# One of four vector sums moved to an accumulating DMA inside SBUF, with the steps put in a new order

## The chip, the cores and the metric

The kernel runs on one core of a Trainium2 chip. The metric is the device time of one execution in microseconds (us); lower is better. Five engines work side by side, each through its own queue of instructions in order: PE (TensorE, matrix products), DVE (VectorE), ACT (ScalarE), POOL (GpSimd) and SP (SyncE). The last two are used here almost only to issue DMA transfers. An engine that has to wait for another holds up everything behind that wait in its own queue.

## The reference

Two parts follow each other: a channel attention over `q`, `k`, `v` (4 batches, 6080 tokens, 256 channels) and a feed-forward block of width 2048 on its result.

```python
qn = q / (np.linalg.norm(q, axis=1, keepdims=True) + 1e-06)
kn = k / (np.linalg.norm(k, axis=1, keepdims=True) + 1e-06)
s = kn.transpose(0, 2, 1) @ qn / tau          # 256 x 256 for each batch
a = softmax(s)
x = (v @ a).reshape(24320, 256)
h = x @ w_in                                  # 24320 x 2048
g = 0.5 * h * (1.0 + np.tanh(c * (h + 0.044715 * h * h * h)))
return g @ w_out                              # 24320 x 256
```

## The kernel before

**The two products.** The attention matrix is multiplied into `w_in` once for each batch (`aw`, 256 x 2048), so that `h = v @ aw` is one product for each block of 512 tokens. There are 12 blocks in a batch, the last of 448 tokens, and 48 in all; `n` is the block's number. The *first product* makes `h` and GELU makes `g` of it (bf16, in SBUF). The *second product* is `g @ w_out`, taken transposed, with `w_out` as the stationary operand.

**Both products use a form of Strassen and Winograd**: a 2 by 2 product of blocks with 7 products in place of 8, for sums that other engines make. In the first product this is done for one to three sets of four feature chunks for each block (the steps `w0...`, `w1...`, `w2...`, among them the matmuls `w0m1` to `w0m7`); the rest is done plainly (`g0`, `g3`, ..., four matmuls of 512 columns each, with GELU `G0`, `G3`, ...). In the second product it is done for all blocks. Write G(f,t) for the quarter of `g` with features half f and tokens half t, and W(h,f) for the quarter of `w_out` with output half h. The kernel before makes on DVE:

- T1 = G(0,1) - G(0,0) (`sums_1`, step `T1a`, one instruction of 2048 elements)
- T2 = G(1,1) - T1, T3 = G(1,1) - G(0,1), T4 = T2 - G(1,0) (`sums_2`, steps `T2a`, `T2b`, `T3a`, ..., two halves of 1024 elements each)

and seven products (`product`, steps `M1A`, `M1B` to `M7A`, `M7B`, four matmuls of 256 columns each): M1 to M3 read `g` itself, M5 reads T1, M6 reads T2, M7 reads T3 and M4 reads T4. The sums of `w_out` are made once at the start (`prep_wout`, steps `pF0`, `pS3`, ...).

**Buffers.** `g` has two buffers of `[128, 16, 512]`, T1, T2 and T3 one each, T4 two. The first GELU of block n+2 can write only when the last reader of block n's `g` is through.

**What sets the order.** Nothing reorders the steps: the list `ORDER` holds one string of steps for each window, a window being the time of one block, and `WINDOW` says which string a block uses (five of them serve twice). The program runs through these strings and hands each step to its engine's queue. A step such as `M7A-1` belongs to the block before. Besides the two products the windows hold the work for the next batch's attention matrix: loads of `q` and `k` (`lq`, `lk`, issued by POOL, with a cast from f32 to bf16), squares on ACT (`qsq`, `ksq`), sums of squares on DVE (`f1` to `f4`), rows of the 256 x 256 Gram matrix on PE (`row0`, ...). `v` is cast to bf16 by a DMA from DRAM to DRAM issued by POOL (`lv`) and then loaded transposed by a DMA issued by SP (`lt`); `vs` makes the sums of it on DVE. A load of `lq`, `lk` or `lv` is held back until the last matmul of a `g` or `w..m` step ahead of it in the list (`GATE`). SP also issues the stores of the output, four for each block.

A set of the first product is a chain across engines: after matmul `m6` DVE adds (`ap`, L618) before `m7` may write the same bank (L597), and ACT copies (`cq`, `y5`) come ahead of that.

**The tail.** After the last matmul of the last block (`M3B` in the last string) DVE still adds (`a12`, L742), transposes (`c12`, `c22`, L751), and four stores (`sA`, L804) go out.

Of the kernel before, what the change touches and what calls it, by code (L numbers as in the profile page):

```python
# [18 lines left out]
def kernel(  # L19
# [75 lines left out]
    def load_one(b, c, which, gate=None):  # L95
        r0, n = chunks_of(b)[c]
        t = qkp.tile([128, 8, 256], BF16, tag="qk"[which])
        src = (q, k)[which]
        after(nc.gpsimd.dma_start(
            out=t[:, 0:n, :],  # L100
            in_=src[b, 0 : R * 128, :].rearrange("(p r) c -> p r c", r=R)[:, r0 : r0 + n, :]), gate)
        if with_rest(b, c):
            after(nc.gpsimd.dma_start(out=t[:REM, n, :], in_=src[b, R * 128 : N, :]), gate)
        qk_tiles.setdefault((b, c), []).append(t)
# [13 lines left out]
    def cast_first(st):  # L118
        for which in range(2):
# [6 lines left out]
            qk_tiles.setdefault((0, 0), []).append(t)  # L126
# [366 lines left out]
    def gs(n):  # L493
        if n not in GS:
            GS[n] = gp.tile([128, FC, BLK], BF16, tag="g", name=f"g{n}")
        return GS[n]
# [32 lines left out]
    def gelu(n, p):  # L529
        cols = cols_of(n)  # L530
        nc.scalar.activation(gs(n)[:, 2 * p : 2 * p + 2, :cols], HP.pop((n, p))[:, :, :cols],  # L531
                             AF.Gelu_apprx_tanh)
# [74 lines left out]
    def set_step(n, i, what):  # L607
# [14 lines left out]
        if what == "Gq":  # L622
            nc.scalar.activation(  # L623
                gs(n)[:, 2 * pa : 2 * pa + 2, :c].rearrange("p u (t x) -> p t u x", t=2),
                QP.pop((n, i))[:, :, :c].rearrange("p t (u x) -> p t u x", u=2),
                AF.Gelu_apprx_tanh)
        if what == "Gr":
            nc.scalar.activation(gs(n)[:, 2 * pb : 2 * pb + 2, :hc], two(RB.pop((n, i))[:, :c]),  # L628
                                 AF.Gelu_apprx_tanh)
        if what == "Gx":  # L630
            nc.scalar.activation(gs(n)[:, 2 * pb : 2 * pb + 2, hc:c], two(XW.pop((n, i))[:, :c]),  # L631
# [24 lines left out]
    def prep_wout(what):  # L656
        if what == "pA11":
            nc.vector.tensor_copy(wc(A11), w_half(0, 0))
        if what == "pF0":
            WF.append(yout.tile([128, 32, 32], FP32, tag="ot", name="wf0"))  # L660
            nc.vector.tensor_add(WF[0], w_half(1, 0), w_half(1, 1))
        if what == "pS1":
            nc.vector.tensor_copy(wc(S1), WF[0])
        if what == "pF1":
            WF.append(yout.tile([128, 32, 32], FP32, tag="ot", name="wf1"))
            nc.vector.tensor_sub(WF[1], WF[0], w_half(0, 0))
# [8 lines left out]
        if what == "pS3":  # L675
            nc.vector.tensor_sub(wc(S3), w_half(0, 0), w_half(1, 0))
# [3 lines left out]
    def quarter(n, f, t, f0=0, f1=8):  # L680
        hc = cols_of(n) // 2
        return GS[n][:, f * 8 + f0 : f * 8 + f1, t * hc : t * hc + hc]
# [6 lines left out]

    def sums_2(n, i, half):  # L690
        hc = cols_of(n) // 2
        ts = TS.setdefault(n, {})
        if i not in ts:
            ts[i] = (t4p if i == 4 else tsp).tile([128, 8, BLK // 2], BF16, tag=f"t{i}",
                                                  name=f"t{i}_{n}")
        f0, f1 = half * 4, half * 4 + 4
        o = ts[i][:, f0:f1, :hc]
        if i == 2:
            nc.vector.tensor_sub(o, quarter(n, 1, 1, f0, f1), ts[1][:, f0:f1, :hc])  # L699
        if i == 3:  # L700
            nc.vector.tensor_sub(o, quarter(n, 1, 1, f0, f1), quarter(n, 0, 1, f0, f1))  # L701
# [6 lines left out]
    def product(n, i, halves=(0, 1), bank=None):  # L708
# [4 lines left out]
        for half in halves:  # L713
# [5 lines left out]
            for k in range(4):  # L719
                fc = half * 4 + k  # L720
                if i <= 3:
                    f, t = {1: (0, 0), 2: (1, 0), 3: (1, 1)}[i]
                    x = GS[n][:, f * 8 + fc, t * hc : t * hc + hc]
# [97 lines left out]
    with tc.manual_schedule():  # L821
# [93 lines left out]
        def step(what, n):  # L915
# [12 lines left out]
            elif what == "T1a":  # L928
                sums_1(n)
            elif what[0] == "T":  # L930
# [38 lines left out]
        for n in range(NN):  # L969
            for x in ORDER[WINDOW[n]].split():  # L970
# [4 lines left out]
WINDOW = [  # L975
    0, 1, 2, 3, 4, 5, 6, 7, 8, 9, 10, 11, 12, 13, 14, 15, 16, 17, 18, 19, 20, 21, 22, 23,
    24, 25, 26, 27, 28, 17, 18, 19, 20, 29, 30, 31, 32, 33, 34, 35, 36, 37, 38, 38, 39,
    40, 41, 42,
]
ORDER = [  # L980
    """g0 lv+3 aw3 G0 aw2 g1 ac2 ac3 aw4 G1 aw5 lq+1 ac4 g2 ac5 g3 G2 aw6 G3 g4 ac6 SW0 aw7 G4 g5
    lk+1 ac7 vtp G5 pA11 g6 vtc0 g7 vtc1 G6 T1a vtq G7""",
    """g0 vtr0-1 vtr1-1 lt+2 lv+3 g1 T2a-1 G0 T2b-1 M1B-1 G1 pF0-1 g2 g3 G2 pS1-1 w0m1+1 pF1-1
    lq+1 M1A-1 G3 g4 cq-1 pS2-1 pNA-1 g5 pS4-1 M6B-1 G5 M5A-1 pS3-1 M6A-1 G4 M5B-1 g7 vs+1
    y5-1 g6 ap-1 G7 T3a-1 lk+1 M3A-1 T3b-1 pA12-1 M7A-1 T4b-1 w0m5+1 M7B-1 w0cq+1 row0 ax-1
    row1 w0y5+1 M3B-1 T4a-1 G6 w0m6+1 M4B-1 c12-1 w0ap+1 M4A-1 qsq M2A-1 c21-1 M2B-1 row2
    c11a-1 M1B ksq T1a w0m2+1 w0m7+1 w0m3+1""",
    """g0 w0Gq T2a-1 lt+2 lv+3 row4-1 M5A-1 w0ax G0 M5B-1 T2b-1 M1A-1 f1-1 g4 cq-1 w0Gx T3a-1
    w0m4 G4 g3 lq+1 f2-1 vs+1 M6A-1 G3 g6 T4b-1 y5-1 M6B-1 c11-2 G6 g5 lt+3 lv+4 ap-1 T3b-1
    w0Gr M3A-1 G5 w0m5+1 T1a w0m1+1 row2 M7A-1 w0cq+1 lk+1 M3B-1 w0y5+1 M7B-1 c12-1 qsq w0m6+1  # L990
    c22-2 g7 w0ap+1 row5-1 T4a-1 row3-1 G7 w0m2+1 ax-1 w0m3+1 w0m7+1 f3-1 M2A-1 ksq M2B-1 T2a""",
    """g0 w0ax w0Gq row5-1 T2b-1 M4A-2 vs+1 M4B-2 G0 w0m4 g4 c21-2 w0Gr c11a-2 f1-1 g3 G4 SW1-3
    M1B-1 lq+1 G3 M5A-1 c22-2 M1A-1 f2-1 w0Gx w1m1 T3b-1 w1m5 M5B-1 w1cq T3a-1 g7 cq-1 T4a-1
    w1y5 lt+3 lv+4 row0-1 w1m6 y5-1 M6A-1 G7 w1ap M6B-1 row1-1 qsq ap-1 w1m2 w1m7 w1m3 w1ax
    row4-1 lk+1 M3A-1 T1a M7A-1 w1Gq w1m4 row3 M7B-1 w1Gr c11-2 M3B-1 f3-1 w1Gx row1 c12-1
    w0m1+1 w0m5+1 T4b-1 row2 w0cq+1 M2B-1 ax-1 M2A-1 w0y5+1 row3-1 ksq c11a-1 w0m6+1""",
    """g0 T3a-1 w0ap M4A-2 G0 M4B-2 T2b-1 M5B-1 T2a-1 w0m7 g3 c21-2 w0ax M1A-1 G3 f4-2 row0-1
    w0m4 M1B-1 c22-2 lq+1 w0Gr T3b-1 w0m3 w0m2 cq-1 w1m5 c11-2 M5A-1 w0Gq f1-1 M6B-1 w1m1 y5-1
    M6A-1 f2-1 w1cq g4 ap-1 lt+3 lv+4 w1y5 T4a-1 w1m6 G4 row4-1 w1ap M3A-1 M7A-1 vs+1 w0Gx
    M3B-1 ksq w1m7 f3-1 lk+1 w1m3 w1ax g7 T4b-1 M7B-1 G7 c12-1 w1m4 row1 ax-1 w1m2 f4-1 M2B-1  # L1000
    w1Gr w0m5+1 w1Gq T1a M2A-1 w0m1+1 M4A-1 w0cq+1 c11a-1 M4B-1 w0y5+1 T2a row5-1 w0m6+1 w1Gx
    M5A c21-1 w0ap+1""",
    """g0 qsq-1 T3a-1 M5B-1 T2b-1 w0m2 G0 M1A-1 f1-1 w0m7 M1B-1 y5-1 w0m3 w0ax cq-1 g3 w0Gq T4b-1
    M6A-1 lq+1 T3b-1 G3 w0m4 g4 vs+1 w0Gr M6B-1 G4 w1m5 ap-1 w1m1 row3-1 f2-1 lt+3 lv+4 row4-1
    w1cq M3A-1 M3B-1 w1y5 w1m6 w0Gx g7 w1ap ksq c12-1 lk+1 row2 w1m2 c22-2 w1m7 w1m3 w1ax
    M2A-1 G7 M7A-1 T4a-1 w1m4 row2-1 f3-1 row0-1 w1Gr M7B-1 T1a w1Gq row5-1 w0m1+1 w0m5+1
    M2B-1 ax-1 w0cq+1 c11-2""",
    """g0 w1Gx-1 T3a-1 w0y5 M4B-2 c11a-2 row0-1 T2b-1 G0 M4A-2 w0m6 c21-2 M5A-1 qsq-1 T2a-1 g3
    w0ap M1A-1 c22-2 M1B-1 f4-2 lq+1 w0m7 cq-1 M5B-1 w0ax G3 row3-1 M6B-1 T4b-1 M6A-1 y5-1
    c11-2 w0m2 w0Gx w0m4 T4a-1 row4-1 w0Gr row1-1 ap-1 w1m5 lt+3 lv+4 w0m3 T3b-1 w1y5 row5-1  # L1010
    w1m1 M3B-1 f1-1 w1cq M3A-1 w0Gq M7B-1 vs+1 w1m6 M7A-1 lk+1 w1ap g4 ksq ax-1 c12-1 w1m7
    w1m2 f2-1 M4B-1 w1ax G4 M4A-1 w1m3 c21-1 M2A-1 w1Gx f3-1 g7 w1Gq f4-1 w1m4 T1a M2B-1 G7""",
    """g0 w1Gr-1 T2a-1 M1A-1 G0 w0m5 c11a-2 w0m1 T4a-1 row3-1 M1B-1 w0cq T3b-1 M5B-1 w0y5 row5-1
    T2b-1 w0m6 cq-1 row0-1 qsq-1 g3 w0ap c11-2 lq+1 row2-1 T3a-1 w0m7 G3 M5A-1 c22-2 w0m2 w0ax
    w0m3 M6A-1 w0Gq T4b-1 M6B-1 w0m4 vs+1 w1m5 y5-1 row1-1 lt+3 lv+4 w0Gr g4 ap-1 w0Gx f1-1
    w1m1 G4 M7A-1 M3B-1 f2-1 M7B-1 w1cq lk+1 M3A-1 w1y5 w1m6 c12-1 qsq g7 w1ap M2B-1 ax-1 w1m7
    G7 c22-1 w1m3 w1m2 w1ax M4A-1 w1Gq T1a M4B-1 w1m4 w0m5+1 w1Gr M2A-1 c21-1 row2 w0y5+1
    c11a-1 row4-1 row4 T3a w0m1+1 M5B w0cq+1 f3-1 M1A T2a w1Gx M1B ksq f4-1 w0m6+1 row3 M5A
    w0ap+1""",
    """g0 c11-2 cq-1 T2b-1 y5-1 w0m7 G0 w0m2 w0ax w0m3 M6A-1 T3b-1 M6B-1 w0Gq g3 ap-1 f1-1 w0Gx  # L1020
    w0m4 G3 g4 vs+1 M7B-1 w0Gr T4a-1 M7A-1 G4 f2-1 w1m5 row1-1 ax-1 w1m1 M3B-1 T1a w1cq row5-1
    M3A-1 lt+3 lv+4 w1y5 w1m6 qsq g7 w1ap c22-1 M4A-1 c12-1 w1m7 ksq row5 w1ax w1m2 row0 row3
    T4b-1 M2A-1 w1m3 f3-1 G7 row2 w1m4 f4-1 M4B-1 M2B-1 w1Gr c21-1 w0m5+1 w1Gq c11a-1 row0-1
    M1B f1 row4 w0m1+1 row1 w0cq+1""",
    """lq+4 g0 f2-1 c11-2 w0y5 f3-1 M5B-1 T2a-1 G0 w0m6 M1A-1 w0ap M5A-1 gc T3a-1 g3 cq-1 w1Gx-1
    f4-1 w0m3 w0m2 T2b-1 w0m7 w0Gq ss w0ax M6B-1 T4a-1 y5-1 G3 M6A-1 sv w0m4 pow ap-1 g4 w0Gr
    T3b-1 w1m5 T4b-1 G4 M3B-1 lt+3 lv+4 w1m1 vs+1 M3A-1 w1cq M7A-1 kf w1y5 lk+4 w1m6 c12-1 g7
    w0Gx w1ap kr M7B-1 T1a G7 w1m7 w1m2 w1m3 krp w1ax w1Gq M2B-1 ax-1 w0m5+1 S0+1 M2A-1 w1Gx
    S1+1 w1m4 th0+1 M4A-1 c11a-1 w1Gr T3a M4B-1 th1+1 M5A c21-1 dn+1 w0m1+1 T2b""",
    """g0 w0cq rc0 w0y5 w0m6 M1B-1 G0 w0ap M5B-1 M1A-1 rc1 y5-1 w0m3 cq-1 w0m7 w0m2 T2a-1 g3 w0Gq  # L1030
    w0ax M6A-1 rc2 G3 lq+4 w0m4 M6B-1 T3b-1 g4 w0Gr ap-1 w0Gx w1m5 rc3 w1m1 lt+3 lv+4 M7B-1
    w1cq M3B-1 c22-2 w1y5 eT w1m6 M3A-1 G4 w1ap rsum+1 M7A-1 T4a-1 w1m7 g7 ax-1 rs+1 w1ax
    aw0+1 G7 c12-1 w1m2 w1m4 vs+1 w1m3 M4A-1 w1Gr ac0+1 M2B-1 w1Gq w0m1+1 T4b-1 w0m5+1 lk+4
    aw1+1 w0cq+1 c11-2""",
# [203 lines left out]
```

## Time and profile before

| | us |
|---|---|
| median of 3 timed runs (696.42 to 696.67) | 696.61 |
| the profiled execution, first to last instruction (its span) | 695.2 |
| median of the timed runs less the span: what lies around it | 1.4 |
| PE busy | 677.3 (97%) |
| DVE busy | 630.8 (91%) |
| ACT busy | 616.0 (89%) |
| POOL busy | 73.4 (11%) |
| DVE, the sums of T3 (L701), 96 instructions | 63.8 |
| mean granted TensorE clock | 0.998 |

The profiled execution has no other time of its own than its span; the 1.4 us between the span and the median is taken as what lies around it. The busy time of PE counts matmuls to their modelled ends, which overlap with the next, so 97% alone does not say that PE runs at its peak. For that one compares the starts of matmuls that follow each other. DMA transfers are shown at the instruction that issues them, with the time from issue to landing. Waits are put down to the engine, line or DMA that ended them.

### The profile page before, as it was taken

Reading aid. Unit: us, or ns where it says so; the run is one execution under the profiler, and the core shown is the slowest. Engines: PE = TensorE matmul, PEld = TensorE weight load, DVE = VectorE, ACT = ScalarE, POOL = GpSimd, SP = SyncE. Lnnn points to the kernel's source line nnn. Section 1 sums busy time; section 2 is a strip of 40 time slices with the busy share of each in tenths; the row PEclk is TensorE's granted clock in tenths of the full one; section 3 lists DMA queues with packets and bytes.
Section 4 is the critical chain, followed back from the end, with each engine's and each line's share of the span. In section 5 each row is a group of like instructions: output and inputs, shape, how many; then the busy total and the mean of one; then the engine's idle time right before and its main releaser. Section 6 shows DMA issues by size and latency. Waiting matters only on the chain.

```text
span 695.2 us, 14413 instructions
## 1 busy us (share of the span) xinstructions
PE 677.3 (97%) x5501; PEld 530.7 (76%) x5501; DVE 630.8 (91%) x1245; ACT 616.0 (89%) x894; POOL 73.4 (11%) x135
## 2 busy tenths in 40 slices
PE   3999999999999999999999999999999999999996
PEld 2857787777778777777777777777877888888785
DVE  3579998999998889999999889999999999999996
ACT  5389989999889999999988999999888999999993
POOL 4321101111001001101010100010000000000000
PEclk9999999999999999999999999999999999999999
DMA  9996888897478777747587777593563463453325
GB/s 240 207 269 98 160 141 126 114 150 109 65 144 126 130 120 105 122 80 121 91 138 121 119 120 126 97 141 53 83 99 69 77 103 61 81 103 59 54 39 89
DMA packets 161462, 79.07 MB, mean 114 GB/s; under 512 B 148448, under 2 KB 152160, under 8 KB 160672
## 3 DMA queue, kind: packets, MB, share of 16 engines
q0 software_dynamic: 14448, 39.72, 34.2%
q1 hardware_dynamic: 145696, 37.14, 31.8%
q10 hardware_dynamic: 1248, 1.28, 0.6%
q8 instruction: 43, 0.70, 0.4%
q14 instruction: 27, 0.22, 0.1%
HBM read 78.91 MB, written 36.57 MB: 166 GB/s over the span
## 4 chain that ended last, share of the span: by engine, by line
PE 95%; DMA 4%; DVE 0%; issue 0%; POOL 0%; ACT 0%; DVEq 0%; POOLq 0%
PE r L726 24%; PE h L521 22%; PE p L726 18%; PE rb L597 13%; PE qp L597 10%; PE G L248 5%; DMA t<-in_k_dram 2%; PE awp L461 2%; DMA t<-in_q_dram 1%; PE ss L282 0%; PE ss L275 0%; PE vt_ps L325 0%; PE rk L406 0%; PE warm L370 0%; DVE vT_pe L331 0%
## 5 line engine op out<-in xcount | busy, mean ns | idle before, releaser
L726 PEld LDWEIGHTS <-wcomb 128*128 128x128 bf16 x2688 | 261.9, 98 | 43.5 <-issue 0.2
L531 ACT ACTIVATE g<-h 128x1024 bf16<-128x1024 f32 (+1 forms) x178 | 179.9, 1014 | 16.4 <-PE h L521 13.9
L726 PE MATMUL r<-t,wcomb 128*128 128x256 bf16 (+1 forms) x1152 | 163.6, 272 | 0.1
L521 PE MATMUL h<-vT,aw 128*128 128x512 bf16 (+1 forms) x624 | 158.6, 377 | 0.0
L623 ACT ACTIVATE g<-qp 128x1024 bf16<-128x1024 f32 (+1 forms) x103 | 104.7, 1016 | 7.3 <-PE qp L597 5.8
L726 PE MATMUL p<-g,wcomb 128*128 128x256 bf16 (+1 forms) x760 | 108.0, 272 | 0.0
L521 PEld LDWEIGHTS <-aw 128*128 128x128 bf16 x712 | 69.2, 98 | 49.4 <-DVE aw L364 0.6
L597 PEld LDWEIGHTS <-sw 128*128 128x128 bf16 x824 | 80.2, 98 | 25.5 <-issue 1.3
L193 ACT ACTIVATE sq<-t 128x1536 bf16<-128x1536 bf16 (+4 forms) x59 | 79.2, 1359 | 6.2 <-DMA t<-in_q_dram 6.0
L618 DVE TENSOR_TENSOR qp<-rb,yw 128x512 f32<-128x512 f32 (+1 forms) x103 | 70.8, 688 | 12.3 <-PE rb L597 9.5
L597 PE MATMUL rb<-tv,sw 128*128 128x256 bf16 (+1 forms) x412 | 78.0, 271 | 0.2 <-DVE qp L618 0.2
L621 DVE TENSOR_TENSOR xw<-rb,yw 128x512 f32<-128x512 f32 (+1 forms) x103 | 69.5, 674 | 3.9 <-PE rb L597 2.4
L613 ACT ACTIVATE qp<-rb 128x512 f32<-128x512 f32 (+1 forms) x103 | 59.7, 580 | 11.9 <-PE rb L597 6.8
L597 PEld LDWEIGHTS <-aw 128*128 128x128 bf16 x618 | 60.3, 98 | 12.7 <-issue 0.7
L631 ACT ACTIVATE g<-xw 128x512 bf16<-128x512 f32 (+1 forms) x103 | 63.4, 626 | 1.3 <-DVE xw L621 1.2
L616 ACT ACTIVATE yw<-qp 128x512 f32<-128x512 f32 (+1 forms) x103 | 61.2, 594 | 3.7 <-PE qp L597 1.9
L699 DVE TENSOR_TENSOR t<-g,t 128x1024 bf16<-128x1024 bf16 (+1 forms) x96 | 63.4, 668 | 0.6
L701 DVE TENSOR_TENSOR t<-g 128x1024 bf16<-128x1024 bf16 (+1 forms) x96 | 63.8, 673 | 0.0
L703 DVE TENSOR_TENSOR t<-t,g 128x1024 bf16<-128x1024 bf16 (+1 forms) x96 | 63.6, 669 | 0.0
L628 ACT ACTIVATE g<-rb 128x512 bf16<-128x512 f32 (+1 forms) x103 | 61.2, 596 | 2.2 <-PE rb L597 1.7
L248 PE MATMUL G<-t 128*128 128x256 bf16 (+1 forms) x352 | 60.1, 279 | 0.1
L687 DVE TENSOR_TENSOR t<-g 128x2048 bf16<-128x2048 bf16 (+1 forms) x48 | 57.5, 1197 | 0.0
(137 smaller groups left out, 890.0 us busy)
## 6 DMA issues: line engine op xcount, KB each, us to landing
out_dram<-ot SPq DMA_DIRECT2D x174, 128.0 KB, 3.2
vb<-in_v_dram POOLq DMA_DIRECT2D x41, 256.0 KB, 4.2
t<-in_q_dram POOLq DMA_DIRECT2D x21, 384.0 KB, 4.9
t<-in_k_dram POOLq DMA_DIRECT2D x21, 384.0 KB, 5.8
wst<-in_moe_w_out_dram POOLq DMA_DIRECT2D x2, 1024.0 KB, 11.0
t<-in_q_dram POOLq DMA_DIRECT2D x3, 512.0 KB, 14.4
t<-in_k_dram POOLq DMA_DIRECT2D x3, 512.0 KB, 17.2
out_dram<-ot SPq DMA_DIRECT2D x12, 112.0 KB, 2.6
```

The source lines that it names most:

```text
L193: nc.scalar.activation(o, t[:np_, r, :], AF.Square)
L248: nc.tensor.matmul(G[b][:, jc, :], lhsT=qt[:np_, r, jc * 128 : jc * 128 + 128], rhs=kt[:np_, r, :], start=first and jc == 0, stop=jc == 1, ...
L521: mm = nc.tensor.matmul(hp[:, u, :cols], lhsT=AW[b][:, cc, fc * 128 : fc * 128 + 128], rhs=vt_tiles[n][:, cc, :cols], start=cc == 0, stop= ...
L531: nc.scalar.activation(gs(n)[:, 2 * p : 2 * p + 2, :cols], HP.pop((n, p))[:, :, :cols], AF.Gelu_apprx_tanh)
L597: GATE[0] = nc.tensor.matmul(acc[:, u * hc : u * hc + hc], lhsT=lhs[:, u * 128 : u * 128 + 128], rhs=rhs, start=m in (1, 5) and u == 0, st ...
L618: nc.vector.tensor_add(qp(n, i)[:, 1, :c], RB[n, i][:, :c], YW[n, i][:, :c])
L621: nc.vector.tensor_add(XW[n, i][:, :c], RB[n, i][:, :c], YW.pop((n, i))[:, :c])
L623: nc.scalar.activation(gs(n)[:, 2 * pa : 2 * pa + 2, :c].rearrange("p u (t x) -> p t u x", t=2), QP.pop((n, i))[:, :, :c].rearrange("p t ( ...
L631: nc.scalar.activation(gs(n)[:, 2 * pb : 2 * pb + 2, hc:c], two(XW.pop((n, i))[:, :c]), AF.Gelu_apprx_tanh)
L701: nc.vector.tensor_sub(o, quarter(n, 1, 1, f0, f1), quarter(n, 0, 1, f0, f1))
L703: nc.vector.tensor_sub(o, ts[2][:, f0:f1, :hc], quarter(n, 1, 0, f0, f1))
L726: nc.tensor.matmul(ACCS[n, acc][:, :hc], lhsT=wcomb[:, w, fc, :], rhs=x, start=first and k == 0, stop=k == 3, skip_group_check=True)
```

## The change

T3 is no longer made by DVE. A DMA that POOL issues reads G(1,1) and adds it to G(0,1) in place, in SBUF, after T1 has read the old G(0,1); M7 then reads that quarter of `g`. The last block (n = 47) keeps T3 on DVE. So that the DMA can add and need not subtract, the signs of the form change: T2 = G(1,1) + T1, T3 = G(1,1) + G(0,1), and the sums of `w_out` follow. `g` is laid out by token halves, `[128, 2, 16, 256]`, so that a quarter of a full block is one run of 2048 elements (4 KB) in each partition. `ORDER` has a string of its own for each of the 48 blocks, all of them different from before, and `q`, `k`, `v` loads may now stand in another order than that of their use (hence `[None, None]` with an index in `load_one`).

```diff
-            GS[n] = gp.tile([128, FC, BLK], BF16, tag="g", name=f"g{n}")
+            GS[n] = gp.tile([128, 2, FC, BLK // 2], BF16, tag="g", name=f"g{n}")
...
-        nc.scalar.activation(gs(n)[:, 2 * p : 2 * p + 2, :cols], HP.pop((n, p))[:, :, :cols],
+        nc.scalar.activation(gs(n)[:, :, 2 * p : 2 * p + 2, : cols // 2],
+                             HP.pop((n, p))[:, :, :cols].rearrange("p u (t x) -> p t u x", t=2),
                              AF.Gelu_apprx_tanh)
...
         if what == "pF0":
-            nc.vector.tensor_add(WF[0], w_half(1, 0), w_half(1, 1))
+            nc.vector.tensor_sub(WF[0], w_half(1, 0), w_half(1, 1))
         if what == "pF1":
-            nc.vector.tensor_sub(WF[1], WF[0], w_half(0, 0))
+            nc.vector.tensor_sub(WF[1], w_half(0, 0), WF[0])
         if what == "pS3":
-            nc.vector.tensor_sub(wc(S3), w_half(0, 0), w_half(1, 0))
+            nc.vector.tensor_sub(wc(S3), w_half(1, 0), w_half(0, 0))
...
     def quarter(n, f, t, f0=0, f1=8):
-        return GS[n][:, f * 8 + f0 : f * 8 + f1, t * hc : t * hc + hc]
+        return GS[n][:, t, f * 8 + f0 : f * 8 + f1, :hc]
...
+    def sum_3(n):
+
+        hc = cols_of(n) // 2
+        nc.gpsimd.dma_start(out=quarter(n, 0, 1), in_=quarter(n, 1, 1), accum_op=ALU.add)
+
     def sums_2(n, i, half):
...
         if i == 2:
-            nc.vector.tensor_sub(o, quarter(n, 1, 1, f0, f1), ts[1][:, f0:f1, :hc])
+            nc.vector.tensor_add(o, quarter(n, 1, 1, f0, f1), ts[1][:, f0:f1, :hc])
         if i == 3:
-            nc.vector.tensor_sub(o, quarter(n, 1, 1, f0, f1), quarter(n, 0, 1, f0, f1))
+            nc.vector.tensor_add(o, quarter(n, 1, 1, f0, f1), quarter(n, 0, 1, f0, f1))
...
-                if i <= 3:
-                    f, t = {1: (0, 0), 2: (1, 0), 3: (1, 1)}[i]
-                    x = GS[n][:, f * 8 + fc, t * hc : t * hc + hc]
+                if i <= 3 or i == 7 and n < NN - 1:
+                    f, t = {1: (0, 0), 2: (1, 0), 3: (1, 1), 7: (0, 1)}[i]
+                    x = GS[n][:, t, f * 8 + fc, :hc]
...
-            for x in ORDER[WINDOW[n]].split():
+            for x in ORDER[n].split():
...
```

The strings of steps are all rewritten. The end of the last one, behind its last first-product matmuls, was and is:

```
before  T2a M5B cq M5A T2b M6A T3a M6B M2B T3b y6 y5 T4b M7A M7B T4a M3A ax M2A M4B c11a M4A c11 M3B c21 a12 sB c12 c22 sA
after   w1m4 w1Gr T4b M6A M6B y6 M5A M5B M7A y5 M7B ax c22 M2B c11a c11 M3A M4A M4B c21 M3B sB a12 c12 sA
```

## The prediction

> **What bounds the kernel now.** I read the page's busy shares first, then PE in stretches, PE's waits, and the starts of neighbouring matmuls, last the DMA landings and the tail.
>
> ```profile
> PE 677.3 (97%) x5501; PEld 530.7 (76%) x5501; DVE 630.8 (91%) x1245; ACT 616.0 (89%) x894; POOL 73.4 (11%) x135
> 0.00:38.00 38.00, 26.46 (x250) 20.45 (x250) 17.74 (x31) 16.82 (x17) 16.95 (x31) 1.00 1.06 223
> 38.00:100.00 62.00, 61.93 (x449) 43.21 (x450) 56.25 (x108) 56.03 (x69) 8.08 (x15) 1.00 0.87 164
> 100.00:600.00 500.00, 499.99 (x4032) 391.94 (x4031) 469.94 (x940) 462.25 (x677) 45.57 (x84) 1.00 0.67 108
> 600.00:689.00 89.00, 88.73 (x774) 75.13 (x771) 85.52 (x168) 80.87 (x133) 2.83 (x5) 1.00 0.37 65
> PE h L521 <- DVE aw L364: 0.4, 1, 0.4
> PE rb L597 <- DVE qp L618: 0.2, 1, 0.2
> ```
>
> The columns of the stretches are length, then busy time of PE, weight loads, DVE, ACT and POOL, the clock and the DMA share. DVE is loaded to 94% between 100 and 600 us, but PE has no gap there at all. Whether a PE without gaps is a full PE shows in the starts:
>
> ```profile
> 304.00 1.04 PE L726 MATMUL r<-t,wcomb 128*128 128x256 bf16 x8
> 304.87 0.38 PE L248 MATMUL G<-t 128*128 128x256 bf16 x2
> ...
> 649.04 0.38 PE L597 MATMUL qp<-tv,sw 128*128 128x256 bf16 x2
> 649.62 0.38 PE L597 MATMUL rb<-tv,sw 128*128 128x256 bf16 x2 [0.20 <-DVE qp L618]
> ```
>
> Eight matmuls of 256 columns take 0.87 us from start to start, 0.109 each. At 649.04 two take 0.58 instead of 0.22: 0.36 us are lost to the DVE addition `ap`, the largest loss of the run. Taken over all neighbouring starts between 38 and 689 us, losses of over 0.06 us come to 3.3 us, some 1.9 of them in front of matmuls that wait for DVE (a dozen, 0.06 to 0.37 each), 0.5 for ACT, the rest at the first 64-row matmul of a batch's Gram row, which waits for nothing. The floor checks this: 4068 matmuls of 256 columns at 0.1093, 708 of 512 at 0.2163, 56 of 448 at 0.190 and 350 of 224 at 0.096 make 642 us, the small ones 4 to 7 us more; 646 to 649 of the 651 us between 38 and 689. So PE's own work sets the time, and the most that a change on other engines can win behind the start is about 3 us, plus what it takes from the tail.
>
> **The change, part by part.**
>
> *PE.* The built programs have the same 5486 matmul instructions of the same shapes. Cost 0, and the floor stays.
>
> *DVE.* 94 additions go, 47 blocks of two, by this row:
>
> ```profile
> L701 DVE TENSOR_TENSOR t<-g 128x1024 bf16<-128x1024 bf16 (+1 forms) x96 | 63.8, 673 | 0.0
> ```
>
> 94 x 0.673 = 63.3 us; DVE falls to about 567 us, 82%. On the path lies only what PE lost to DVE, 1.9 us. I take 1.7 of it as won (ends 0 and 1.9; near the upper, since the additions it waits for then stand in a queue with 1.3 us more room for each 13.9 us block). If that stall goes, ACT at 89% is late next, with 0.5 us.
>
> *Layout and signs.* GELU writes 1024 elements in 1014 ns in one run (L531) and 1016 ns rearranged (L623); T2 reading one quarter of `g` and a dense T1 takes 668 ns, T3 with two quarters 673. Subtractions become additions of the same shape. Ends: -0.2 to +0.2 us; taken 0, hidden by PE.
>
> *POOL.* 47 more issues of 0.50 to 0.57 us (rows L153, L99) make 24 to 27 us; POOL goes to 15%. T3 on POOL waits for the block's last GELU of tokens half 1 and for T1. Behind it stand the next `lq`, `lk`, `lv`; squares on ACT and `lt` on SP wait for those. The lists give `lq` 9.6 us or more of PE work before `qsq` (before: 16.5) and `lk` 15.0 (13.7), against landings of 4.4/5.1/7.2 us (least, median, most, 100 to 640 us). Cost 0, ends 0 and 2.
>
> *The new wait.* M7 now waits on PE for T3's landing, with everything on PE behind it, so any lateness is lost in full. I walked the lists, adding the start-to-start times above for each PE step, and measured from the end of what T3 waits for (GELU 1.0 us, 0.63 for L631, T1 1.2 us by its row, or the POOL issue ahead) to M7's first matmul. Over 47 blocks the room is 7.1 us at least (block 30), under 8.4 in eight blocks, 9.4 in the median and 13.1 at most. No row shows an accumulating DMA. The nearest:
>
> ```profile
> t<-in_q_dram POOLq DMA_DIRECT2D x21, 384.0 KB, 4.9
> t<-in_k_dram POOLq DMA_DIRECT2D x21, 384.0 KB, 5.8
> wst<-in_moe_w_out_dram POOLq DMA_DIRECT2D x2, 1024.0 KB, 11.0
> DMA to landing us min/median/max: 4.4/5.1/7.2
> ```
>
> T3 writes 512 KB. Between the 384 KB loads (mean 5.35) and the 1024 KB load, by size, it lands after 5.35 + 5.65 x 128 / 640 = 6.5 us. The lower end is 4.4 us, the fastest 384 KB load; the upper 11.0, as if reading source and destination made it a 1 MB load. Lateness summed over the blocks: 0 us up to a landing of 7.0, 2.3 at 8, 5.7 at 8.5, 11.3 at 9, 38 at 10, 75 at 11. I take 6.5 us and a cost of 0, with 0.3 for early blocks: at 38 to 100 us the DMA share is 0.87, and T3 of blocks 0, 1 and 4 comes up to 5 us behind loads from POOL issued just ahead.
>
> The Trainium skill's page "Collectives: The Full Stack" (The bandwidth ceiling) says that an add by DMA costs nothing in arithmetic but reads two sources, and so runs at half the rate of a copy. No row here shows that; taken at its plainest, twice the 5.1 us of a 384 KB load, it would put T3 near 10 us, an estimate, and the sum near +38 us.
>
> A rule against this change: a POOL DMA's descriptors are written by GpSimd, and DVE instructions in certain modes lock it out. The row first: the 45 `vb` issues took 486/505/558 ns on POOL while DVE was 94% busy. The skill's "SBUF — State Buffer" (SBUF: two separate sides) tells of this trap; with these issue times I give it 0, and by the rule each T3 would slip behind DVE work of about 1 us, which the room of 7.1 us still holds.
>
> *SP and `lt`.* Loads in free order shorten leads: from `lv` to `vs` the lists have 11.3 us in block 4, then 19.1 and more (before: 28.4 and more). Needed are 0.5 + 4.5 + 4.8 = 9.8 us in the medians; at worst, with the longest landings 10.7 and 9.4, 20.6. Ends 0 and 9 us; I take 0.1, near the medians.
>
> *Start and tail.* The code up to 38 us is the same. At the end:
>
> ```profile
> 688.63 0.55 PE L726 MATMUL p<-g,wcomb 128*128 128x224 bf16 x4
> 689.21 0.39 DVE L742 TENSOR_TENSOR c<-p,y 128x224 f32<-128x224 f32 x1
> 689.64 0.70 DVE L751 STREAM_TRANSPOSE ot<-c 128x224 f32<-128x224 f32 x2
> ```
>
> Two transposes stand ahead of the last stores; `c22` moves in front of `M3B`, and one of about 0.4 remains: -0.3 us (ends 0 and -0.4).
>
> *Sum*, against the profiled execution: 695.2 - 1.7 (DVE waits) + 0.3 (early T3) + 0.1 (`lt`) - 0.3 (tail) = 693.6, and with the 1.4 us around it 695.0. The new lists also fill some of ACT's 0.5; I take 0.3: **694.7 us**.
>
> **The rivals.**
> - *T3 lands late.* For it: two reads for one write, and a room of 8.7 to 9.4 in many blocks, so that the price climbs steeply. Against: loads of 384 KB never took over 7.7 us past 100 us. It decides from a landing of 8.2 us (more than 2.5 us of lateness, which eats the gain). At 9 us: 694.7 + 11.3 = 706; at 10 us 732.
> - *PE was full and stays so:* new small stalls, of a few tenths each in the 48 new windows, replace the 1.9 us. Before had a dozen in 48; the same again gives 696.6, within +-1.4.
> - *A load in free order comes late* (block 4's `v`, or `lq` with 9.6 us) and holds PE up once or twice: +2 to +6, 699 to 703.
> - *All goes:* every loss of 3.3 us except the 64-row ones (about 0.6), and 0.4 in the tail: 693.5.
>
> That the sum isn't moved at all is excluded: the built program has 885 DVE additions and subtractions in place of 979, and 173 POOL transfers in place of 126.
>
> **How the numbers follow.** A measurement tells some 0.2% from no change, 1.4 us: faster is under 695.2, slower over 698.0. Forecast and "all goes" together 0.55 (692.5 to 695.8, of it 0.53 under 695.2); PE stays full 0.17; T3 late 0.18; a late load 0.10. Faster 0.53, same 0.18, slower 0.29. The low end of the range, 692.5, is all losses gone and 1 us more; the high end must hold the late loads and the mild half of late T3s, so 705; what lies beyond, T3 landings of about 9 us and more, is about 0.12. The forecast alone has 692.5 to 696.
>
> **What would show it.** Right: DVE near 567 us; POOL near 98; PE waits on DVE under 0.1 us; T3's DMA from issue to landing 6 to 7 us in the median and under 8 nearly always; no PE wait on line 694 or on `g`; starts of matmuls 0.109 apart throughout; one transpose behind the last matmul. Wrong: PE waits put down to the DMA `g<-g`, or M7's first matmul half a microsecond and more behind its neighbour, above all in blocks 30, 20, 16 and 44; DMA share over 0.9 in mid run with landings of `vT` over 7 us; losses in front of `rb` and `qp` matmuls as large as before.

## The result and the profile after

The changed kernel takes 748.39 us (median of 4 runs, 739.87 to 763.02) against 696.55 for the kernel before (696.42 to 696.67): a ratio of 1.070 with a 95% interval of 1.064 to 1.077. Medians here are of all runs, while the ratios leave out those over 1.5% above the fastest of their kernel (here 763.02; without it the median is 746.06, and each difference from 748.4 below is 2.3 us smaller). It is slower by 52 us, where 1.9 us less had been predicted. Its times also spread, over 11 us even without that run, those of the kernel before over 0.3. The profiled execution is the fastest of the four, 739.87 us with a span of 738.1, so the two traces differ by 42.9 us.

The page of the changed kernel: busy shares, the clock over 40 slices of 18.5 us, and the queue of POOL's transfers.

```profile
PE 681.3 (92%) x5426; PEld 533.6 (72%) x5501; DVE 587.9 (80%) x1151; ACT 614.9 (83%) x894; POOL 119.3 (16%) x182
...
PEclk9999999999999999999589999989999999999999
...
q0 software_dynamic: 23904, 64.17, 50.4%
```

DVE is relieved as meant. PE is busy for 92% of a longer span, with a dip of the clock near 350 us. The POOL queue moved 64.17 MB (before: 39.72). By stretches (length, busy time of PE, weight loads, DVE, ACT, POOL, then clock, DMA share, GB/s):

```profile
38.00:100.00 62.00, 55.31 (x378) 37.34 (x384) 45.30 (x84) 50.11 (x60) 12.85 (x20) 0.97 0.98 193
100.00:300.00 200.00, 192.72 (x1528) 151.17 (x1551) 167.37 (x330) 179.15 (x256) 35.99 (x55) 1.00 0.89 149
300.00:400.00 100.00, 80.28 (x613) 61.25 (x622) 71.74 (x145) 71.39 (x107) 11.40 (x17) 0.90 0.88 115
400.00:600.00 200.00, 195.43 (x1543) 153.56 (x1566) 168.41 (x339) 177.79 (x263) 28.79 (x41) 0.98 0.77 128
```

PE, which had no gap at all between 100 and 600 us, now lacks 20 us in one stretch of 100 us and some 7 at the start. Its waits between 38 and 733 us name the cause (us in total, times, longest):

```profile
PE r L732 <- DMA g<-g: 25.2, 5, 19.2
PE G L248 <- DMA t<-in_q_dram: 7.3, 2, 4.5
PE r L732 <- DVE t L705: 1.4, 1, 1.4
```

The first line is M7 (L732 with `g` as the moving operand) waiting for T3, five times, and once for 19.2 us. The second is a Gram row that waits for a load of `q`. Measured in the starts of neighbouring matmuls, as the prediction did, ten losses of over 0.6 us make 36.7 us: 19.4 at 349.8 us, 4.7 at 54.7, the rest of 0.6 to 2.9 each. The kernel before had none. T3's own landings (line L694; the second line is issue to landing, least, median, most):

```profile
L694 POOL DMA_DIRECT2D g<-g x47: 850/893/1636, 49.6 to 713.7; - x47
...
DMA to landing us min/median/max: 4.5/6.2/27.2
```

The median, 6.2 us, fits the room of 7.1 us and more that the lists give. But 11 of the 47 took over 8 us, four of these over 10, and one of the four 27.2. That one, in the timeline (start, length, engine, line):

```profile
340.15 4.97 SPq L163 DMA_TRANSPOSE vT<-vb  x1
...
341.34 0.53 POOL L99 DMA_DIRECT2D t<-in_k_dram  x1 [2.51 <-PE h L521]
342.12 0.88 POOL L694 DMA_DIRECT2D g<-g  x1 [0.25 <-ACT g L531]
346.57 0.55 POOL L99 DMA_DIRECT2D t<-in_q_dram  x1 [3.57 <-PE rb L598]
347.68 0.53 POOL L99 DMA_DIRECT2D t<-in_k_dram  x1 [0.56 <-PE rb L598]
...
369.34 1.03 PE L732 MATMUL r<-g,wcomb 128*128 128x256 bf16 x4 [19.20 <-DMA g<-g]
```

A transposing load of `vT` and a load of `k` are under way when T3 is issued at 342.12, and two more loads join. None of these five lands in under 24 us. All DMA of the core between 345 and 365 us, with the time from issue to landing on the last line:

```profile
DMA packets 1055, 0.77 MB, mean 38 GB/s; under 512 B 890, under 2 KB 890, under 8 KB 1055
...
vT<-vb SPq DMA_TRANSPOSE x1, 27.7
```

38 GB/s, where the 40 us ahead moved 139. I call this a collapse: three microseconds or more in a row under 75 GB/s while packets hold the engines for over three quarters of the time. The stretches show that, and how the clock adds to the loss:

```profile
340.00:345.00 5.00, 4.95 (x39) 3.72 (x39) 4.86 (x9) 3.61 (x6) 1.41 (x2) 1.00 2.85 175
345.00:350.00 5.00, 4.95 (x43) 4.04 (x42) 4.76 (x12) 4.64 (x9) 1.68 (x3) 1.00 0.33 20
350.00:355.00 5.00, 0.14 (x1) 0.00 (x0) 1.91 (x6) 1.15 (x2) 0.42 (x1) 0.83 0.49 23
355.00:360.00 5.00, 0.00 (x0) 0.00 (x0) 0.00 (x0) 0.00 (x0) 0.00 (x0) 0.50 1.31 48
...
370.00:380.00 10.00, 9.95 (x63) 6.97 (x63) 6.83 (x16) 6.99 (x13) 2.24 (x4) 0.81 0.82 151
```

The DMA share of the four rows from 340 to 360 us averages 1.2 (a packet's time is counted where it starts): packets are in flight all the time and take long. The clock falls to 0.50 within some 5 us of the stall (by single microseconds, at 353.3). After it the four matmuls from 369.34 take 0.83 us from start to start of their groups, 0.21 each in place of 0.109, and full speed is back at 373.8: some 2.2 us more. The Trainium skill's page "TensorE: Matmul & The Clock Gate" (Part 1) tells of a clock halved after an idle window of about 3.4 us and restored after a busy one of that length. Here the clock fell 3.2 us after PE stopped (350.1 to 353.3), which agrees, and came back 4.4 us after PE started again at 369.34, a microsecond more.

### The profile page after: what moved, and what is told of

Its sections match the earlier page's. It is cut to its first block, busy times and chain, and to the rows that moved or that the text cites. A ratio compares the mean times of both kernels' runs of the same rounds, so it can differ in the third digit from the quotient of the medians.

```text
span 738.1 us, 14343 instructions
## 1 busy us (share of the span) xinstructions
PE 681.3 (92%) x5426; PEld 533.6 (72%) x5501; DVE 587.9 (80%) x1151; ACT 614.9 (83%) x894; POOL 119.3 (16%) x182
## 3 DMA queue, kind: packets, MB, share of 16 engines
q0 software_dynamic: 23904, 64.17, 50.4%
## 4 chain that ended last, share of the span: by engine, by line
PE 75%; DMA 17%; issue 4%; DVE 1%; POOL 1%; ACT 1%; POOLq 0%; DVEq 0%
PE r L732 20%; PE h L521 16%; PE p L732 14%; PE rb L598 11%; DMA g<-g 9%; PE qp L598 8%; PE G L248 4%; DMA t<-in_k_dram 4%; DMA t<-in_q_dram 3%; PE awp L461 1%; POOL t L99 1%; DMA vT<-vb 1%; DVE qp L619 0%; DVE t L709 0%; PE ss L275 0%
## 5 line engine op out<-in xcount | busy, mean ns | idle before, releaser
L732 PEld LDWEIGHTS <-wcomb 128*128 128x128 bf16 x2688 | 264.0, 98 | 70.4 <-DMA g<-g 19.7
L531 ACT ACTIVATE g<-h 128x1024 bf16<-128x1024 f32 (+1 forms) x178 | 179.8, 1015 | 32.3 <-PE h L521 29.2
L521 PE MATMUL h<-vT,aw 128*128 128x512 bf16 (+1 forms) x561 | 153.8, 378 | 3.3
L732 PE MATMUL r<-g,wcomb 128*128 128x256 bf16 (+1 forms) x760 | 106.9, 273 | 25.4 <-DMA g<-g 25.2
L624 ACT ACTIVATE g<-qp 128x1024 bf16<-128x1024 f32 (+1 forms) x103 | 104.5, 1015 | 13.8 <-PE qp L598 13.0
L732 PE MATMUL r<-t,wcomb 128*128 128x256 bf16 (+1 forms) x776 | 107.4, 274 | 1.4 <-DVE t L705 1.4
L732 PE MATMUL p<-g,wcomb 128*128 128x256 bf16 (+1 forms) x760 | 105.2, 273 | 0.0
L598 PEld LDWEIGHTS <-sw 128*128 128x128 bf16 x824 | 80.1, 98 | 24.7 <-issue 2.5
L694 POOL DMA_DIRECT2D g<-g x47 | 44.5, 947 | 250.7 <-ACT g L632 50.4
L622 DVE TENSOR_TENSOR xw<-rb,yw 128x512 f32<-128x512 f32 (+1 forms) x103 | 69.8, 678 | 16.2 <-PE rb L598 14.2
L598 PE MATMUL rb<-tv,sw 128*128 128x256 bf16 (+1 forms) x412 | 77.8, 271 | 0.3
L598 PEld LDWEIGHTS <-aw 128*128 128x128 bf16 x618 | 60.7, 98 | 16.3 <-issue 0.7
```

Source lines behind the costliest of these rows:

```text
L521: mm = nc.tensor.matmul(hp[:, u, :cols], lhsT=AW[b][:, cc, fc * 128 : fc * 128 + 128], rhs=vt_tiles[n][:, cc, :cols], start=cc == 0, stop= ...
L531: nc.scalar.activation(gs(n)[:, :, 2 * p : 2 * p + 2, : cols // 2], HP.pop((n, p))[:, :, :cols].rearrange("p u (t x) -> p t u x", t=2), AF ...
L598: GATE[0] = nc.tensor.matmul(acc[:, u * hc : u * hc + hc], lhsT=lhs[:, u * 128 : u * 128 + 128], rhs=rhs, start=m in (1, 5) and u == 0, st ...
L622: nc.vector.tensor_add(XW[n, i][:, :c], RB[n, i][:, :c], YW.pop((n, i))[:, :c])
L624: nc.scalar.activation(gs(n)[:, :, 2 * pa : 2 * pa + 2, :hc], QP.pop((n, i))[:, :, :c].rearrange("p t (u x) -> p t u x", u=2), AF.Gelu_app ...
L732: nc.tensor.matmul(ACCS[n, acc][:, :hc], lhsT=wcomb[:, w, fc, :], rhs=x, start=first and k == 0, stop=k == 3, skip_group_check=True)
```

## The experiments

All ran beside the kernel before (696.5 to 696.7 in each group). "T3's quarter" is the quarter of `g` that M7 reads.

### The new order and T3, one at a time

**T3 by DVE, at T3's place in the new list.**

```diff
-        nc.gpsimd.dma_start(out=quarter(n, 0, 1), in_=quarter(n, 1, 1), accum_op=ALU.add)
+        nc.vector.tensor_add(quarter(n, 0, 1), quarter(n, 0, 1), quarter(n, 1, 1))
```

> The changed kernel with T3 made by DVE (one in-place addition of 2048 elements, some 1.2 to 1.3 us, at the place of T3 in the list); order, layout and signs stay as changed. Theory S (the accumulating transfer is the cause: beside other transfers it sometimes holds all DMA engines up): no landing over 10 us past 100 us, no PE wait of several us, 695 to 705 us, runs within 0.3% of each other. Rival O (the free order of the loads is the cause): still over 720 us, with landings of vT and t over 10 us and runs that scatter.

758.37 us (755.02 to 760.28), ratio 1.088 (1.084 to 1.091). PE now waits for DVE in many places (for T3 9.1 us in six, for `c` and the additions around `ap` some 20 more), up to 3 us each. DVE takes its steps in order, and at a place chosen for another queue the 1.20 us addition waits for the last GELU with all DVE work behind it. The new list only makes sense with T3 off DVE, so this says nothing on the DMA.

**T3 left out** (M7 reads its quarter without the sum).

```diff
-        nc.gpsimd.dma_start(out=quarter(n, 0, 1), in_=quarter(n, 1, 1), accum_op=ALU.add)
+        return
```

> The changed kernel with T3 left out altogether: M7 reads the old G(0,1), so the output is wrong by that sum; neither DVE nor a DMA makes it. It gives the time of the new order with a T3 that costs nothing. Theory S: 693 to 696 us. Rival O: over 720 us as in the changed kernel.

706.30 us (705.04 to 707.87), ratio 1.014 (1.012 to 1.016). With T3 for nothing the new order is still 9.7 us slower than before:

```profile
PE G L248 <- DMA t<-in_q_dram: 4.6, 2, 4.0
PE G L248 <- DMA t<-in_k_dram: 1.8, 2, 1.4
```

Gram rows wait for loads that are issued in a bunch; those between 46 and 54 us take 10 to 14 us to land. Neither theory had this: it is 10 us over Theory S's range and 14 under Rival O's.

**T3 as a plain copy** of G(1,1) over T3's quarter, without the sum (`accum_op` taken out).

> T3 as a plain DMA copy of G(1,1) over G(0,1) from the same queue, of the same 512 KB, with the same waits; nothing is added, so M7's product is wrong. If it is the accumulation that hurts (two reads for one write, 0.33 us for a 4 KB packet): landings near 4 us, no collapse, 694 to 700 us. If any further 512 KB transfer at that place hurts: 715 to 750 us with landings of over 15 us somewhere.

725.85 us (717.39 to 732.69), ratio 1.038 (1.031 to 1.044). Copies land after (least, median, most)

```profile
DMA to landing us min/median/max: 2.8/4.6/17.3
```

and additions after 4.5/6.2/27.2. The copy's longest landing and its stall of 9.5 us come at 341 and 349 us, the same place. So a further transfer of this size costs 19.6 us over no T3, and the addition 22.5 more. The packets show what the addition does: one of 4096 bytes takes 160 ns in the median as a copy and 329 as an addition (both past 100 us).

**T3 kept, the transposing loads of `vT` replaced by plain loads** of the same bytes (so `vT` holds them untransposed).

```diff
-        nc.sync.dma_start_transpose(out=vT[:, :, :cols], in_=v_bf.pop(n)[:cols, :])
+        nc.sync.dma_start(out=vT[:, :, :cols], in_=v_bf.pop(n)[:cols, :].rearrange(
+            "t c -> (t c)").rearrange("(p u x) -> p u x", p=128, u=2))
```

> The changed kernel, accumulating T3 included, with the transposing loads of v replaced by plain loads of the same bytes from SP (v reaches the products untransposed, so the output is wrong). If the accumulating transfer collapses beside a transposing one (in the slow stretch from 343 to 365 us both were in flight): no landing over 12 us, 694 to 702 us. If the transposing loads have no part in it: 715 to 750 us, with collapses as before.

717.13 us (715.27 to 719.84), ratio 1.030 (1.027 to 1.032). T3's landings (from issue, as above) are the same in the median and not at the end, and no collapse is left in the trace:

```profile
DMA to landing us min/median/max: 4.5/6.2/13.7
```

So 31 of the 52 us go with the transposes, though T3 moves every byte that it moved before. The 694 to 702 expected for this case is missed: 20.5 us stay. The plain loads also move other packets: past 100 us some 5,600 of 2048 and 896 bytes stand for 40,000 of 256. The runs don't tell whether the transposing itself or the many small packets do the harm.

**Both: no T3, plain loads.**

> The changed order, T3 left out, and the transposing loads of vT replaced by plain loads of the same bytes. Without T3 the new order lost 9.7 us, 4.2 of them where a Gram row waits for q at 55 us. If these come from cast loads that stand behind transposing loads: 695 to 699. If they come from the bunched cast loads alone: the wait at 55 us stays, 701 to 707.

704.76 us (704.34 to 705.44), ratio 1.012 (1.010 to 1.013). The wait of the Gram row for `q` at 55 us is there, 4.0 us: what the new order costs by itself isn't due to the transposes. With this run the table of the new order is full:

| new order, us | transposing loads | plain loads |
|---|---|---|
| no T3 | 706.3 | 704.8 |
| T3 by DMA | 748.4 | 717.1 |

T3 beside plain loads adds 12.4, the transposes without T3 1.5; together they add 43.6. The 29.7 us beyond the sum of the two come only where the program has both.

### The old order

**The new code with the old order**: before's list, T3's DMA put behind the last of what it waits for.

```diff
- ... T2a-1 g3 w0Gq w0ax M6A-1 rc2 G3 lq+4 w0m4 M6B-1 T3b-1 g4 w0Gr ...   (string 10, before)
+ ... T2a-1 g3 w0Gq w0ax M6A-1 rc2 G3 lq+4 w0m4 M6B-1 g4 w0Gr ...
```

> The new code with the old order of steps (each block's two T3 steps taken out, the accumulating DMA put right behind the last of what it waits for). Walking the list, M7 stands 3.6 us behind T3's inputs at least, 7.5 in the median. Theory C (T3's DMA collides with transposing loads and bunched loads; with the old, spread loads it lands in 4.5 to 6.5 us as a rule): lateness of 2 us (landings of 4.5) to 18 us (landings of 6 everywhere), so 697 to 715, no single stall over 5 us, no landing over 12 us. Theory D (an extra accumulating DMA beside transposing loads is enough by itself, whatever the order): landings over 15 us here too, stalls of 10 us and more, 730 or more. If the landings fit and the wait in short rooms hurts little: under 697.

712.19 us (709.63 to 713.03), ratio 1.022 (1.020 to 1.024). DMA share is 0.87 from 100 to 600 us, more than in the changed kernel, yet no landing of T3 is over 10.8 us and no stall over 2.5:

```profile
PE r L732 <- DMA g<-g: 11.3, 13, 2.3
```

**The same with T3 left out.**

> As the run with the old order, T3 left out altogether: M7 reads the quarter of g without the sum. It tells what 63 us less on DVE are worth when nothing else changes. The prediction's step for DVE (1.7 us of PE waits won) gives 694.5 to 695.5. The rival that PE stays full gives 696.0 to 697. If the new layout or the signs cost something, over 697.5.

696.44 us (696.09 to 696.55, 10 runs), ratio 0.9998 (0.9989 to 1.0007): no difference. DVE is down to 84%, and nothing comes of it. The waits of weight loads ahead of the first product's matmuls, in which the prediction saw DVE at fault, before (L597):

```profile
PEld L597 <- issue: 2.0, 9, 0.4
```

and without T3 (the same line, now L598):

```profile
PEld L598 <- issue: 1.9, 8, 0.4
```

With 63 us of DVE's work gone they stay, and the longest, 0.4 us, stands at the same step (649 us). So they are no queue on DVE; the time of the chain itself (matmul `m6`, addition `ap`, matmul `m7`) is left.

**T3 onto a scratch tile that nobody reads**, in both orders: the same bytes, no wait of M7 (which reads its quarter without the sum).

```diff
+    scr = const.tile([128, 8, BLK // 2], BF16, name="scr")
+    nc.vector.memset(scr, 0.0)
...
-        nc.gpsimd.dma_start(out=quarter(n, 0, 1), in_=quarter(n, 1, 1), accum_op=ALU.add)
+        nc.gpsimd.dma_start(out=scr[:, :, :hc], in_=quarter(n, 1, 1), accum_op=ALU.add)
```

> The run with the old order of steps and T3's DMA, again onto a scratch tile that nobody reads. With the wait it lost 15.7 us against before, without the DMA nothing. Theory W: 696 to 698. Theory L: 702 to 712.

Old order: 699.88 us (696.58 to 708.70, 10 runs), ratio 1.006 (1.002 to 1.010), between the two theories. Most of the 15.7 us is M7's wait; the traffic alone costs at most 1.1 us in half of the executions and 5 to 12 us in the others. The trace is of one of the first half (696.93), so what the others wait for is not seen.

> The changed kernel, its accumulating DMA moved as many bytes at the same places, but adds G(1,1) onto a scratch tile that nobody reads, so that M7 waits for nothing (its quarter of g stays without the sum). Theory W (the loss is M7's wait for T3): close to the run without T3, 704 to 712. Theory L (the loss is that T3's bytes make the loads of q, k and vT late, and PE waits for those): 720 to 750, with waits in front of Gram rows and first-product matmuls.

New order: 735.60 us (724.88 to 737.65), ratio 1.047 (1.040 to 1.055), inside Theory L's range but by another way than it said. ACT's longest waits between 330 and 380 us:

```profile
ACT g L531 <- DMA scr<-g: 14.8, 1, 14.8
```

and PE's longest wait:

```profile
PE h L521 <- ACT g L531: 14.5, 1, 14.5
```

T3 is issued at 339 us, takes 29.6, and holds G(1,1) as its source; the GELU that is to write that buffer for block n+2 waits, and PE behind it. The collapse comes whether M7 waits or not, and finds another way to PE.

**Old order, T3, plain loads of `vT`.**

> The run with the old order and T3's DMA (712.2), the transposing loads of vT replaced by plain loads of the same bytes. In the new order that replacement took 748 to 717 with T3 and 706 to 705 without. If long landings of T3 come from the transposing loads in this order too: no landing over 8 us, 699 to 704, what is left being the short rooms. If in this order the short rooms alone cost the 15.7 us: 709 to 713.

709.22 us (708.08 to 709.45), ratio 1.018 (1.016 to 1.019). In the old order the transposes make 3.0 of the 15.7 us (less whatever plain loads save there without T3, which no run shows; in the new order it was 1.5). Most of the 12.7 left are M7's waits in short rooms (3.6 us at least) for a DMA that never lands in under 4.5:

```profile
PE r L733 <- DMA g<-g: 9.2, 9, 2.6
```

### Size and places

**Half of T3** (four of eight feature chunks, 256 KB; the other half without the sum).

```diff
+        nc.gpsimd.dma_start(out=quarter(n, 0, 1, 0, 4), in_=quarter(n, 1, 1, 0, 4), accum_op=ALU.add)
```

> The changed kernel with only half of T3 added (four of eight feature chunks, 256 KB in place of 512 KB; the other half stays without the sum). If the loss goes with the bytes beside the transposing loads: T3's median landing 3.5 to 5 us, its longest under 15, and the time between the run without T3 (706) and the full one (748), 712 to 730. If a collapse comes with any accumulating DMA: 735 or more.

715.72 us (710.95 to 719.36), ratio 1.027 (1.023 to 1.032); landings 3.2/4.7/12.8 us. Half the bytes cost 9.4 us over no T3, all of them 42.1: far from linear.

**The loads at the places that the old order gave them** in PE's work, the other steps in the new order (31 of 138 loads earlier than that, since the new order needs them sooner).

> The changed kernel with its order of matmuls, vector and scalar steps, but the loads of q, k, v and vT put back to where the old order had them in PE's work (31 of 138 earlier, by 2 to 52 us, since the new order uses them earlier), and T3's DMA listed right behind its inputs, so that M7 stands 7.1 us or more behind them, as in the changed kernel. Theory C (the new order's bunched loads make the long landings): most of the 52 us goes, 697 to 712, T3's longest landing under 15 us and the stall at 350 us gone. Theory D (T3 beside transposing loads is enough): 730 to 755, with a T3 landing over 15 us somewhere.

728.43 us (719.65 to 730.27), ratio 1.042 (1.035 to 1.049): better by 20 us than the changed kernel, short of what Theory C gave and near Theory D. M7's room is the same as in the changed kernel. The stall at 350 us is gone; new ones of 6.0, 5.5, 3.9 and 3.6 us stand at 59, 304, 267 and 82 us, T3's longest landing is 16.2 (Theory D: over 15).

> As the run with the loads put back, T3 left out. With the changed order as it was this lost 9.7 us against the kernel before. If the places of the loads are what costs those (a Gram row that waits 4.2 us for q at 55 us, 1.5 at 287), 694.5 to 698. If the order of the other steps costs them (stalls on DVE or ACT), 703 to 707.

Without T3: 705.62 us (699.12 to 707.26), ratio 1.011 (1.007 to 1.016); not the 694.5 to 698 that places alone should have given. This profile has a collapse with no T3 in it, between 54 and 67 us, and PE stands 5.8 us, from 66.0, in front of a Gram row that waits for `q` (all DMA from 45 to 85 us, slices of 1 us):

```profile
GB/s 374 410 197 203 202 209 312 137 148 33 27 34 38 54 46 57 23 47 13 26 47 27 184 210 213 144 204 201 208 191 195 348 35 172 185 140 97 10 385 98
...
t<-in_q_dram POOLq DMA_DIRECT2D x3, 384.0 KB, 20.0
...
vT<-vb SPq DMA_TRANSPOSE x3, 19.4
```

Eight loads of `q`, `k` and `v` were issued within some 12 us beside two transposing loads. T3 is thus not needed for a collapse; it is one more transfer of the kind that makes one.

**A few loads moved.** Thirteen in all: nine at the start put in the order of use and spaced, four around 340 us spread over the empty stretch behind. The first string, in part:

```diff
-g0 lv+3 aw3 ... g3 pA11 lq+2 lk+5 aw7 ac7 G2 lv+7 aw6 ... pS3 lq+1 g6 G6 vtc0 lk+2 M1B ...
+g0 lv+3 aw3 ... g3 lq+1 pA11 aw7 ac7 G2 aw6 ac6 G3 g4 G4 g5 lq+2 G5 ... pS3 g6 lk+2 G6 ...
```

> The changed kernel with 13 loads moved within its list and nothing else: nine at the start put in the order of their use and spaced (the two early loads for blocks 5 and 7 later), and four of the loads of q and k that stand around 340 us spread over the empty stretch behind. Theory B (the stalls at 55 and 350 us come from too many POOL transfers in flight beside a transposing load, and where the loads stand decides): both stalls gone, 712 to 728, T3's longest landing under 16 us. Rival R (long landings turn up somewhere whatever the places, since T3 adds 24 MB): another stall of 10 us and more elsewhere, 732 to 755.

732.85 us (727.01 to 743.10), ratio 1.049 (1.042 to 1.056). The stalls at 55 and 350 us are gone, and one of 9.3 us stands elsewhere, at 191 us (Rival R gave 10 and more), behind a T3 of 17.3 us with two transposing loads and four loads around it:

```profile
PE r L732 <- DMA g<-g: 15.5, 6, 9.2
PE r L732 <- DVE t L705: 5.7, 2, 4.0
```

> The changed kernel with only the four loads around 340 us moved. Theory B: the stall at 350 us gone, the one at 55 us of 4 to 5 us there as before, 718 to 732. Rival R: 736 to 755, with a stall of 10 us or more at another place.

Only the four around 340 us: 733.96 us (729.11 to 745.47), ratio 1.051 (1.047 to 1.056). That lies between the two theories: the stall at 350 us is gone, but one of 8.5 us stands at 192. So the one bunch at 340 us was worth some 14 us of the median; the rest is spread over many places.

> The changed order without T3, with only the nine loads at the start moved. Without T3 the order as it was took 706.3, with 4.2 us of them in front of a Gram row at 55 us that waits for a load of q. Theory B: that wait under 1 us, 700.5 to 703. If the bunch at the start costs nothing by its order: 705 to 707.

Only the start, without T3: 705.29 us (702.04 to 710.27), ratio 1.013 (1.009 to 1.018). In the profiled execution (702.04) the Gram row's wait of 4 us is gone, but the median is only 1 us better than with the bunch. The places at the start explain the wait, not the 9.7 us. What else the new order costs without T3 is open: small waits of Gram rows, one of M6 for T2 of 2 us, and a spread of 8 us between executions.

### What the transposing loads show

From issue and landing of every transposing load after 40 us, in twelve runs with transposing loads and T3's DMA whole or absent (540 in all; the thirteenth such run, with only the loads around 340 us moved, gives the same picture), by what else was in flight from its issue to 3 us after:

| loads of `q`, `k`, `v` in flight | without T3: count, median, most (us) | with T3: count, median, most (us) |
|---|---|---|
| 0 | 158, 3.6, 5.3 | 84, 4.8, 10.1 |
| 1 | 91, 4.9, 7.6 | 36, 7.2, 13.2 |
| 2 | 69, 6.5, 16.7 | 30, 9.8, 28.9 |
| 3 | 32, 8.7, 21.1 | 10, 10.9, 27.7 |
| 4 and more | 19, 12.1, 26.1 | 11, 16.4, 21.9 |

A transposing load with one load beside it takes 1.3 us longer in the median. With three transfers from POOL, T3 among them or not, the medians are 8.7 and 9.8 us and the worst over 20. Collapses by the measure above stand in 11 of the 15 traces with transposing loads, each time with such a load in flight, and in none of the three with plain loads. That the meeting of these streams lengthens landings is what the traces show; why it does is not settled here. The Trainium skill's page "DMA: Bandwidth & Descriptors" (Rules for kernel authors) says of transposes next to ordinary DMAs that they need nothing. That speaks of the data being right; for the time the table shows what company costs.

None of these versions beats the kernel before. The free T3 in the old order, 696.44, bounds what the idea can bring there: nothing.

## Why the prediction was wrong

- **The new wait** is the step that failed. It took one landing time for all T3s, 6.5 us, from loads that landed in 4.4 to 7.7 us past 100 us in the trace of before, and set it against the least room, 7.1: cost 0. The median was right (6.2), in part by luck: it was scaled by size from casting loads out of DRAM, and the same bytes copied within SBUF landed after 4.6. But a landing depends on what else is in flight. The changed list puts T3 beside transposing and bunched loads, 11 of 47 landings passed the 8 us that "nearly always" was to hold, and one took 27.2. T3 costs 42.1 us in this order (748.4 against 706.3), 29.7 of them by the meeting with transposing loads. The walk of the lists asked how long M7 could wait; it never asked what was in flight at T3's issue.
- **POOL, and SP and `lt`**, were given 0 and 0.1 us (ends to 2 and 9). They set leads against landings of the old order ("4.4/5.1/7.2", at worst 10.7 and 9.4). The new order's bunches lengthen those landings to 10 to 16 us around 50 us, and without T3 it loses 9.7; not all of that is explained. (The 4.5 in the sum for `lt` is the median of casts and transposes taken together; the casts alone landed after 4.2.) POOL's issue of T3 takes 0.95 us (44.5 us for 47), not 0.50 to 0.57, and POOL comes to 119 us, not 98; no wait of PE in the profile is put down to that.
- **DVE**: 588 us against some 567 predicted, 80% against 82: the 63 us of instructions went, but they overlap with their neighbours, and busy time counts an overlap once (without T3 in the old order the durations add up to 643 us, before to 707, while busy time is 580 and 631). The 1.7 of 1.9 us taken as won did not come: in the old order with T3 free the same waits are 1.9 of 2.0. They stay with the chain `m6`, `ap`, `m7`. The rival "PE stays full" had this right.
- **Layout and signs**: 0, and right. GELU takes 1015 ns and the old order without T3 is equal to before within 0.1%.
- **Tail**: from the start of the last matmul to the end 6.1 us against 6.3, -0.2 where -0.3 was predicted.
- **The rival "T3 lands late"** (0.18) had the side, "two reads for one write", but as one later time for all blocks: 706 at 9 us. The sizes came otherwise: a median that fits and a tail of landings that grows with company. The rule cited beside it from the page "Collectives: The Full Stack" (The bandwidth ceiling), which the page gives for the reducing step of ring collectives, is borne out in the packets: 329 ns for an added one of 4096 bytes, 160 for a copied one. The whole landing does not double: at best 4.5 us against 2.8 for the copy, 1.6 times. Half of T3 landed in 3.2 us at best, so by an estimate from these two runs some 1.9 of the 4.5 us do not grow with the bytes. Near 10 us, the estimate put beside the rule, is off: it doubled the whole landing of a cast load from DRAM.
- **The range** ended at 705. Even without T3 the order is past it.

## What to carry to other kernels

A transfer's landing time, read in a trace, holds for the company that it had there; before a wait is hung on a DMA, list what will be in flight at its issue in the new order, and keep transposing loads out of a crowd of transfers from the POOL queue (moving loads alone won 14 to 20 of the 52 us here). Price the tail of the landings, not the median, wherever the tensor engine waits in order. And before an engine is relieved, take the work away altogether once: if the time stays (here 696.44 against 696.53), no cheaper place for that work can win in that order.

## What the runs showed that was not expected

- Collapses of all DMA of the core while the DMA engines are busy, to 36 GB/s for 19 us with T3 and for 13 us without it, only in traces with transposing loads; in the two longest three and more transfers from POOL were in flight beside one.
- 512 KB added in place in SBUF land after 4.5 us at best, 512 KB copied after 2.8, 256 KB added after 3.2; the issue on POOL takes 0.95 us for the addition and 0.57 for the copy. An added packet takes twice the time of a copied one.
- A read by a late DMA stalls as hard as a write: on the scratch tile T3 still cost PE 14.5 us, through the buffer that it read.
- Steadiness is lost even where M7 waits for nothing: executions lie 8 to 12 us apart in the old order with T3 onto scratch and in two runs of the new order without T3; in the kernel before they lie 0.3 apart, in the old order without T3 0.5.
